# Sliding-window attention and a feed-forward layer on one core: PSUM banks by row tile, one phase of sums, output banks by row of tokens

## The chip, the cores and the metric

The kernel runs on one core of one Trainium2 chip. The metric is the device time of one execution in microseconds (us). Three executions of the kernel before took 361.39 to 361.45 us, the median is 361.41 us. Instructions are queued in order on five engines: TensorE (PE, with its weight loads listed apart as PEld), VectorE (DVE), ScalarE (ACT), GpSimd (POOL) and SyncE (SP). PE writes to PSUM, which has eight banks of 512 float32 columns on 128 partitions; DVE and ACT read it.

## The reference, cut to what matters

Eight batches of eight heads, 576 positions, head dimension 64; each position sees the positions up to 32 away. The result, as 4608 tokens of 512 values, goes through two matrices with a piecewise function between.

```python
scores = np.matmul(q, k.transpose(0, 1, 3, 2)) / np.sqrt(D)
mask = np.abs(pos[:, None] - pos[None, :]) <= 32
attn = softmax(np.where(mask, scores, -1e9))
x = np.matmul(attn, v)                 # -> tokens (4608, 512)
h = x @ w_in                           # (512, 2048)
g = np.where(h >= 1, h, np.where(h <= -1, 0.0, (h + 1) ** 2 / 4))
out = g @ w_out                        # (2048, 512)
```

## The kernel before

**Attention.** Heads come in pairs `h` (0 and 1), four pairs `y` per batch. Keys go in chunks `c` of 64, nine per head. For each chunk, `scores` multiplies 64 keys by the 128 queries around them (L194); ACT takes the exponent (L201), DVE or POOL multiplies with a band mask (L202), and the masked weights stay in `pt`. The last chunk has 96 queries and its own function `scores8` (L210, L213, L214). Every one of these matmuls uses a quarter of the PE array: 64 rows by 64 columns. The row half holds the head in `scores`; in the sums it holds the parity of the chunk.

**Sums.** `Sums` takes a range of queries (256, 224 or 96 wide) of two pairs of heads, or of four for the last 96, and forms for each head the sum of weights times `vn` and the sum of weights times `ones`, with 64 by 64 matmuls (L217) into a tile `bb` of two PSUM banks: bank 0 for the weighted sums, bank 1 for the row sums. Both row halves of the array add into each bank. So the work is in two phases: in phase 0 the low row half adds to bank 0 and the high half to bank 1, in phase 1 the other way round. Between the two stands a DVE copy of one number out of the bank, `scr` (L273), and phase 1 begins behind it. `end` takes the logarithm of the row sums (L280), the exponent of its negative (L281) and queues a DVE product (L283) that writes `xT`; `flush` issues it at the beginning of the next slot.

**Main loop.** 144 slots (`a`), eight for each tile of 256 tokens, and then slots that finish the output. A slot has eight matmuls of 256 columns (L392) into a bank `hp`, out of two banks in turn; ACT makes `rr` (L400), and DVE makes `gT` out of both (L401, L402). The second matrix follows `LAG` = 8 slots behind: four matmuls of 512 columns (L416) into `op`, one tile of two banks, one bank for each 128 tokens. Each slot gives two matmuls to either bank. In the eighth slot of a tile the first bank gets its last two matmuls, ACT copies it to `osb` (L420), then the second bank gets its two, and ACT copies that one; SP sends both out. The next tile needs `op` in the slot after.

**What sets the order.** `ev` holds for a slot which sums and which scores run there; the list `sl` gives 35 slots three or four apart, each with one `Sums` and, but for two of them, the `scores` of a later step. I call such a slot an event. In an event slot the program order is: the eight L392, phase 0, `scores`, phase 1, `end`, the four L416; an event with no scores puts phase 0 ahead of the L392. Slots 8 to 11 and 19 to 21 also transpose q and k of batches 1 and 2 on PE (L171): q, its copy by ACT, then k into the same PSUM tile, and its copy by DVE (L172). Batches 0 and 1 are loaded in long rows, two pairs of heads at a time (`load_long`), and put in order by a copy (`relay`, L145; batch 1 on POOL, queued behind the loads that POOL issues). All loads are issued from POOL and share a ring of semaphores.

**Before the first slot**, all scores of batch 0 and the sums of its first 256 queries run, in two `Sums`.

Of the kernel before, what the change touches and what calls it, by code (L numbers as in the profile page):

```python
# [15 lines left out]
def kernel(  # L16
# [19 lines left out]

# [34 lines left out]
    scr = const.tile([128, 8], FP, name="scr")  # L71
# [11 lines left out]
    def load_long(b, qd, t):  # L83

        src, dst, nm = ((q, qn, "qn"), (k, kn, "kn"))[t]
        if qd == 0:
            dst[b] = nat.tile([128, 2, 2, S], BF, name=nm, tag=nm)
        rows = src[b].rearrange("(h y) s d -> h (y s) d", h=2)[:, 2 * qd * S:2 * qd * S + 2 * S]
        nc.gpsimd.dma_start(out=dst[b][:, qd], in_=rows.rearrange("h (x j) d -> x h (j d)", j=NC))

    def load_nat(b, t):
        src, dst, nm = ((q, qn, "qn"), (k, kn, "kn"), (v, vn, "vn"))[t]
        x = dst[b] = nat.tile([128, NU, 2, D], BF, name=nm, tag=nm, bufs=3 if t == 2 else 2)
        for h in range(2):
            nc.gpsimd.dma_start(out=x[:, :, h], in_=src[b, NY * h:NY * h + NY].rearrange("y s d -> (y s) d")  # L95
                                .rearrange("(u p) d -> p u d", p=128))

# [27 lines left out]
    load_nat(0, 2)  # L125
# [9 lines left out]
    load_nat(1, 2)  # L135
# [19 lines left out]
    def tpose(b, n, t, copy, ps):  # L155
# [3 lines left out]
        if b < LONG:  # L159
            qd, part = divmod(n, 2)  # L160
            j0, j1 = ((0, 5), (5, 9))[part]
            src = (qj, kj)[t][b, qd]
            dst = o.rearrange("d (y p j) -> d y p j", p=64, j=NC)[:, 2 * qd:2 * qd + 2, :, j0:j1]
            i = ps[:, :j1 - j0].rearrange("d j (g p) -> d g p j", g=2)
# [7 lines left out]
        copy(dst, i)  # L172
# [9 lines left out]
    def half(n):  # L182
        return HD[n % 2]

    def scores(b, ys, cs, eng, pool=ps_s):

        if b not in pt:
            pt[b] = ptp.tile([128, 2, NY, 512], BF, name="pt")
        ps = two_banks(pool)
        n = 0  # L190
        for y in range(*ys):
            for c in range(2 * cs[0], 2 * cs[1]):
                for h in range(2):
                    nc.tensor.matmul(ps[half(NC * y + c), h, 128 * (n // 2):128 * (n // 2) + 128],  # L194
                                     kT[b][HD[h], S * y + 64 * c:S * y + 64 * c + 64],
                                     qTs[b % 3][HD[h], PAD + S * y + 64 * c - 32:PAD + S * y + 64 * c + 96],
                                     start=True, stop=True)
                n += 1
        p = pt[b][:, :, ys[0]:ys[1], 128 * cs[0]:128 * cs[1]]
        like = "p h (y j) -> p h y j"  # L200
        A.activation(p, ps[:, :, :64 * n].rearrange(like, y=ys[1] - ys[0]), AF.Exp, scale=D ** -0.5)  # L201
        eng.tensor_mul(p, p, mask4[:, :128 * n].rearrange("p (h j) -> p h j", h=2).rearrange(like, y=ys[1] - ys[0]))  # L202

    def scores8(b, eng):

        p = pt8[b] = ptp.tile([128, 2, 2 * TAIL], BF, name="pt8")
        ps = two_banks(ps_s)
        for y in range(NY):
            for h in range(2):
                nc.tensor.matmul(ps[half(y), h, TAIL * (y // 2):TAIL * (y // 2) + TAIL],  # L210
                                 kT[b][HD[h], S * y + 512:S * y + 576],
                                 qTs[b % 3][HD[h], PAD + S * y + MAIN:PAD + S * y + S], start=True, stop=True)
# [3 lines left out]
    def mm(o, w, x, first):  # L216
        nc.tensor.matmul(o, w, x, skip_group_check=True, start=first[0], stop=True)  # L217
        first[0] = False

    muls = []  # L220

    class Sums:


        def __init__(self, b, ys, lo, hi, pool=ps_n):
            self.b, self.ys, self.lo, self.hi = b, ys, lo, hi
            self.bb = two_banks(pool)
            self.firsts = [[[True], [True]], [[True], [True]]]

        def parts(self, y, par):  # L230

            b, lo, hi = self.b, self.lo, self.hi
            R = half(NC * y + par)
            if lo == MAIN:
                c = 7 if par else 8
                yield c, lo, lo + (64 if par else TAIL), lambda h: (
                    pt[b][R, h, y, 448:512] if par else pt8[b][R, h, TAIL * (y // 2):TAIL * (y // 2) + TAIL])
                return
            for c2 in range(4):
                a0, a1 = max(0, 128 * c2 - 32 + 64 * par, lo), min(128 * c2 + 96 + 64 * par, hi)  # L240
                if a0 < a1:
                    yield 2 * c2 + par, a0, a1, lambda h, a0=a0, a1=a1: (
                        pt[b][R, h, y, a0 + 32 - 64 * par:a1 + 32 - 64 * par])

        def phase(self, n):

            b, lo, hi = self.b, self.lo, self.hi
            todo = []
            for y in range(*self.ys):
                off = (y - self.ys[0]) * (hi - lo) - lo  # L250
                for lowhigh in range(2):
                    R = HD[lowhigh]
                    par = (NC * y + lowhigh) % 2
                    got = list(self.parts(y, par))
                    bank = n ^ lowhigh
                    if bank == 1 and len(got) > 1:
                        a0, a1 = got[0][1], got[-1][2]
                        got = [(None, a0, a1, lambda h, a0=a0, a1=a1, par=par, R=R, y=y: (
                            pt[b][R, h, y, a0 + 32 - 64 * par:a1 + 32 - 64 * par]))]
                    for m, (c, a0, a1, p) in enumerate(got):  # L260
                        for h in range(2):
                            w = ones[R] if bank else vn[b][R, (NC * y + c) // 2, h]
                            todo.append(((y, bank == 0 and m + 1 == len(got), m), bank, lambda bank=bank, h=h, w=w, p=p, a0=a0, a1=a1, off=off: mm(
                                self.bb[HD[h], bank, off + a0:off + a1], w, p(h), self.firsts[bank][h])))
            todo.sort(key=lambda x: x[0])
            if n:
                todo.reverse()
            for _, _, f in todo:
                f()
            if n == 0:  # L270

# [47 lines left out]
    x.phase(1)  # L319
    x.end()  # L320
    flush()
    x = Sums(0, (2, 4), 0, TB, ps_o)
    x.phase(0)
    scores8(0, V)
    x.phase(1)
# [134 lines left out]
```

## Time and profile before

| | |
|---|---|
| median of three runs | 361.41 us |
| the profiled execution, its own time | 363.6 us |
| its span, first to last instruction | 361.9 us |
| PE busy | 308.1 us, 85% |
| DVE busy | 246.7 us, 68% |
| ACT busy | 192.0 us, 53% |
| POOL busy | 126.4 us, 35% |

Times within the trace count from the start of the span. A row of the list of instructions in order of time begins with start and length in us, then engine, line, operation, output and inputs and a count; brackets behind it give the idle time of the engine before it and what ended that. The lengths of matmuls include a modelled end, so how fast a row of them goes is read from the starts of two rows that follow each other.

### The profile page before, as it was taken

What the parts mean: (1) busy time and instruction counts of PE and PEld (TensorE: products, weight loads), DVE (VectorE), ACT (ScalarE), POOL (GpSimd) and SP (SyncE); (2) the same over time, 40 slices, a digit from 0 to 9 for tenths busy, and PEclk for the clock granted to TensorE, in tenths of its full rate; (3) what the DMA queues carried; (4) which work ended last, traced back from release to release, by engine and by line L of the source; (5) the groups of instructions that cost most, each with busy time, mean ns of one, the idle gap of its engine ahead of it and who ended that gap; (6) DMA issues with size and microseconds to landing.
All of it is one profiled execution on the core that took longest, in us unless ns stands there. A gap on an engine that the chain in (4) does not pass through costs nothing.

```text
span 361.9 us, 8161 instructions
## 1 busy us (share of the span) xinstructions
PE 308.1 (85%) x3465; PEld 206.6 (57%) x3508; DVE 246.7 (68%) x398; ACT 192.0 (53%) x314; POOL 126.4 (35%) x106
## 2 busy tenths in 40 slices
PE   2667778777989898989898989899979899999985
PEld 1445555455666566656565656565646565655642
DVE  2648778566687768777687777786748777778750
ACT  2645437554556555557655566556454756543331
POOL 8655900141623482238321844139221242100000
PEclk9999999899999999999999999999989999999999
DMA  7999997192909999899981699109950101010111
GB/s 103 179 205 207 178 152 35 60 115 17 126 0 189 68 144 55 184 95 85 110 159 58 45 157 187 60 1 146 172 124 7 60 2 61 0 60 1 61 58 58
DMA packets 127845, 34.22 MB, mean 95 GB/s; under 512 B 117056, under 2 KB 123200, under 8 KB 127808
## 3 DMA queue, kind: packets, MB, share of 16 engines
q0 software_dynamic: 99264, 18.35, 67.7%
q1 hardware_dynamic: 28544, 15.34, 17.5%
q8 instruction: 27, 0.44, 0.5%
q14 instruction: 10, 0.08, 0.1%
HBM read 36.70 MB, written 9.44 MB: 127 GB/s over the span
## 4 chain that ended last, share of the span: by engine, by line
PE 70%; ACT 12%; DVE 10%; issue 6%; DMA 1%; POOL 0%; ACTq 0%; POOLq 0%
PE hp L392 32%; PE bb L416 30%; PE bb L217 6%; DVE hp L401 3%; ACT rr L400 3%; DVE gT L402 3%; ACT osb L420 3%; PE tp L171 2%; ACT qT L172 2%; ACT lr L280 1%; DVE scr L273 1%; DMA kn<-in_k_dram 1%; ACT rc L281 1%; ACT pt L201 1%; DVE xT L283 1%
## 5 line engine op out<-in xcount | busy, mean ns | idle before, releaser
L416 PE MATMUL bb<-w_out,gT 128*128 128x512 bf16 x533 | 143.9, 383 | 22.8 <-ACT osb L420 17.5
L392 PE MATMUL hp<-xT,w_in 128*128 128x256 bf16 x1152 | 154.2, 278 | 4.9 <-DVE gT L402 3.3
L400 ACT ACTIVATE rr<-hp 128x512 f32<-128x512 f32 x144 | 85.9, 597 | 130.6 <-PE hp L392 125.7
L392 PEld LDWEIGHTS <-w_in 128*128 128x128 bf16 x1152 | 113.7, 100 | 48.9 <-issue 4.6
L401 DVE TENSOR_TENSOR hp<-hp,rr 128x512 f32<-128x512 f32 x144 | 100.8, 700 | 57.6 <-ACT rr L400 54.8
L402 DVE SCALAR_TENSOR_TENSOR gT<-rr,hp 128x512 bf16<-128x512 f32 x144 | 99.0, 687 | 4.9
L202 POOL TENSOR_TENSOR pt<-pt,mask 128x1024 bf16<-128x1024 bf16 x24 | 51.2, 2133 | 116.6 <-ACT pt L201 110.3
L416 PEld LDWEIGHTS <-gT 128*128 128x128 bf16 x576 | 53.6, 98 | 62.1 <-issue 24.0
L283 DVE TENSOR_TENSOR xT<-bb,rc 128x512 bf16<-128x512 f32 (+2 forms) x40 | 25.5, 637 | 19.4 <-ACT rc L281 19.3
L217 PE MATMUL bb<-pt,vn 64*64 64x64 bf16 (+3 forms) x712 | 31.4, 213 | 6.7 <-DVE scr L273 4.6
L217 PEld LDWEIGHTS <-vn 64*64 64x64 bf16 x712 | 25.0, 111 | 18.0 <-issue 17.9
L201 ACT ACTIVATE pt<-bb 128x1024 bf16<-128x1024 f32 (+1 forms) x33 | 32.8, 997 | 1.7 <-PE bb L194 1.7
L420 ACT COPY osb<-bb 128x512 f32<-128x512 f32 x36 | 20.9, 582 | 19.4 <-PE bb L416 19.4
L217 PE MATMUL bb<-pt,ones 64*64 64x256 bf16 (+4 forms) x384 | 30.8, 257 | 0.0
L214 POOL TENSOR_TENSOR pt<-pt,mask 128x384 bf16<-128x384 bf16 x7 | 6.4, 915 | 56.6 <-ACT pt L213 56.6
L281 ACT ACTIVATE rc<-lr 128x512 f32<-128x512 f32 (+2 forms) x40 | 23.5, 587 | 1.3
L280 ACT ACTIVATE lr<-bb 128x512 f32<-128x512 f32 (+2 forms) x40 | 22.0, 551 | 2.6 <-PE bb L217 2.0
L95 POOL DMA_DIRECT2D vn<-in_v_dram x16 | 19.6, 1238 | 1.9 <-DMA w_out<-in_moe_w_out_dram 1.3
L194 PE MATMUL bb<-qT,kT 64*64 64x128 bf16 x512 | 13.6, 228 | 1.8 <-DVE qj L145 0.8
L95 POOL DMA_DIRECT2D qn<-in_q_dram x12 | 14.9, 1244 | 0.0
L95 POOL DMA_DIRECT2D kn<-in_k_dram x12 | 14.7, 1238 | 0.0
L217 PEld LDWEIGHTS <-ones 64*64 64x64 bf16 x384 | 13.6, 108 | 1.9 <-issue 1.9
(40 smaller groups left out, 92.2 us busy)
## 6 DMA issues: line engine op xcount, KB each, us to landing
out_dram<-osb SPq DMA_DIRECT2D x36, 256.0 KB, 2.0
qn<-in_q_dram POOLq DMA_DIRECT2D x16, 288.0 KB, 6.0
kn<-in_k_dram POOLq DMA_DIRECT2D x16, 288.0 KB, 8.0
vn<-in_v_dram POOLq DMA_DIRECT2D x16, 288.0 KB, 9.6
w_in<-in_moe_w_in_dram POOLq DMA_DIRECT2D x8, 256.0 KB, 10.8
w_out<-in_moe_w_out_dram POOLq DMA_DIRECT2D x4, 512.0 KB, 13.5
qT<-qn SPq DMA_TRANSPOSE x5, 5.9
kT<-kn SPq DMA_TRANSPOSE x5, 4.7
```

The lines of the kernel that those rows point to most:

```text
L95: nc.gpsimd.dma_start(out=x[:, :, h], in_=src[b, NY * h:NY * h + NY].rearrange("y s d -> (y s) d") .rearrange("(u p) d -> p u d", p=128))
L201: A.activation(p, ps[:, :, :64 * n].rearrange(like, y=ys[1] - ys[0]), AF.Exp, scale=D ** -0.5)
L202: eng.tensor_mul(p, p, mask4[:, :128 * n].rearrange("p (h j) -> p h j", h=2).rearrange(like, y=ys[1] - ys[0]))
L217: nc.tensor.matmul(o, w, x, skip_group_check=True, start=first[0], stop=True)
L281: A.activation(rc[:, :n], lr[:, :n], AF.Exp, scale=-1.0)
L283: muls.append(lambda: V.tensor_mul(xT[:, self.ys[0]:self.ys[1], r0:r0 + w], self.bb[:, 0, :n].rearrange("p (y j) -> p y j", y=ny), rc[:, : ...
L392: nc.tensor.matmul(hp[:, j], w_in[:, kk, 256 * f + 128 * j:256 * f + 128 * j + 128], xT[:, kk, r0:r0 + TB], start=kk == 0, stop=kk == 3)
L400: A.activation(rr, hp, AF.Relu, scale=0.5, bias=0.5)
L401: V.tensor_max(hp, hp, rr)
L402: V.scalar_tensor_tensor(gT[t][:, 2 * f:2 * f + 2], rr, 1.0, hp, op0=ALU.min, op1=ALU.mult)
L416: nc.tensor.matmul(op[:, tt], gT[t][:, ff, 128 * tt:128 * tt + 128], w_out[:, ff], start=ff == 0, stop=ff == 2 * NF - 1)
L420: A.copy(osb, op[:, tt])
```

## The change

In `sums`, which takes the place of the class, a row half of the array stands for one of two pairs of heads (`y1` and `y1 + 2`) in place of the parity of the chunk. Each row half has a bank of its own, with the weighted sums in the first columns and the row sums behind them. So there is one phase, no `scr` copy, and one stretch of matmuls in front of the scores. `scores`, `scores8`, the loads of q, k (batches 0 and 1) and v are re-laid to suit: those DMAs are split by halves of the partitions, two for each that was there.

`op` becomes a tile of one bank for 128 tokens, filled by sixteen matmuls in four slots in a row, out of two banks in turn; the copy to `osb` comes once in four slots. `LAG` goes from 8 to 12, `gT` has three buffers. In the slots before the twelfth, the two banks of `op` serve as third and fourth bank for `hp`. Before the first slot only those scores of batch 0 run that its first 256 queries need; the others go to slots 0 to 2, and the remaining sums to slots 3, 4 and 6 (before: 1, 1 and 4). The transposes of q and k in a slot are issued together, ahead of both copies.

```diff
-    def __init__(self, b, ys, lo, hi, pool=ps_n):
-            ...
-            if n == 0:
-                col = (self.ys[1] - self.ys[0]) * (hi - lo) - (1 if lo < MAIN else TAIL)
-                V.tensor_copy(scr[64:65, 0:1], self.bb[64:65, 0, col:col + 1])
+    def sums(b, y1, lo, hi, pool=ps_n):
+        bb = two_banks(pool)
+        ...
+        for n, (c, c0, c1, p) in enumerate(todo):
+            o = D0 if c is None else 0
+            for a in range(2):
+                for h in range(2):
+                    nc.tensor.matmul(bb[HD[h], a, o + c0:o + c1], ones[HD[a]] if c is None else vn[b][HD[a], c, h],
+                                     p(a, h), start=n == 0, stop=True, skip_group_check=True)
+        def end():
+            ...
+            A.activation(lr[:, :, :D0], bb[:, :, D0:2 * D0], AF.Ln)
+            A.activation(rc[:, :, :D0], lr[:, :, :D0], AF.Exp, scale=-1.0)
 ...
-    LAG = 8
+    LAG = 12
 ...
-    at(1, (0, (0, 2), TB, MAIN), None)
-    at(1, (0, (2, 4), TB, MAIN), None, ps_o)
-    at(4, (0, (0, NY), MAIN, S), None)
+    at(0, None, (0, (0, 2), (1, 2), (2, 4)))
+    at(1, None, (0, (0, 2), (0, 1), (3, 4)))
+    at(2, None, (0,))
+    at(3, (0, 0, TB, MAIN), None)
+    at(4, (0, 1, TB, MAIN), None)
+    at(6, (0, 0, MAIN, S), None)
 ...
-            hp = ps_h.tile([128, 2, TB], FP, name="hp", tag="hp")
+            if a < LAG and a % 4 > 1:
+                hp = ps_o.tile([128, 2, TB], FP, name="hp", tag="op")
+            else:
+                hp = ps_h.tile([128, 2, TB], FP, name="hp", tag="hp")
 ...
-            t, f = divmod(a - LAG, NF)
-            if f == 0:
-                op = two_banks(ps_o)
-            for tt in range(2):
-                for ff in (2 * f, 2 * f + 1):
-                    nc.tensor.matmul(op[:, tt], gT[t][:, ff, 128 * tt:128 * tt + 128], w_out[:, ff],
-                                     start=ff == 0, stop=ff == 2 * NF - 1)
-                if f == NF - 1:
+            for x in range(4 * (a - LAG), 4 * (a - LAG) + 4):
+                tt, ff = divmod(x, 2 * NF)
+                if ff == 0:
+                    op = ps_o.tile([128, DM], FP, name="op", tag="op")
+                nc.tensor.matmul(op, gT[tt // 2][:, ff, 128 * (tt % 2):128 * (tt % 2) + 128], w_out[:, ff],
+                                 start=ff == 0, stop=ff == 2 * NF - 1)
+                if ff == 2 * NF - 1:
                     osb = osp.tile([128, DM], FP, name="osb")
-                    A.copy(osb, op[:, tt])
+                    A.copy(osb, op)
 ...
-            for x in range(2):
-                tpose(b, n, x, (A.copy, V.tensor_copy)[x], tp[:, x])
+            copies = [tpose(b, n, x, (A.copy, V.tensor_copy)[x], tp[:, x]) for x in range(2)]
+            for x in copies:
+                x()
```

Two places show how the queues of ACT and DVE move. The first is ACT at slot 103, an event in which a tile of the output also ends (`pt` is the exponent of scores, `lr` and `rc` belong to the sums, `osb` to the output, `rr` to the slots). Before:

```order
L400 ACTIVATE rr<-hp 128x512 x4
L201 ACTIVATE pt<-bb 128x2x2x256
L280 ACTIVATE lr<-bb 128x512
L281 ACTIVATE rc<-lr 128x512
L420 COPY osb<-bb 128x512 x2
L400 ACTIVATE rr<-hp 128x512 x3
```

After, from the event of slot 99 to the one of slot 103:

```order
L210 ACTIVATE pt<-bb 128x2x2x256
L263 ACTIVATE lr<-bb 128x2x224
L264 ACTIVATE rc<-lr 128x2x224
L406 COPY osb<-op 128x512
L388 ACTIVATE rr<-hp 128x512 x4
L210 ACTIVATE pt<-bb 128x2x2x256
L263 ACTIVATE lr<-bb 128x512
L264 ACTIVATE rc<-lr 128x512
L406 COPY osb<-op 128x512
L388 ACTIVATE rr<-hp 128x512 x3
```

Two copies behind one event have become one copy every four slots; at this place it still stands behind the three of the event and ahead of the next `rr`.

The second is DVE in the slots 0 to 3, from the last product for `xT` before slot 0 on. Before:

```order
L283 TENSOR_TENSOR xT<-bb,rc 128x2x256
L401 TENSOR_TENSOR hp<-hp,rr 128x512
L402 SCALAR_TENSOR_TENSOR gT<-rr,hp 128x512
L273 COPY scr<-bb 1x1 x2
L401 TENSOR_TENSOR hp<-hp,rr 128x512
L402 SCALAR_TENSOR_TENSOR gT<-rr,hp 128x512
L283 TENSOR_TENSOR xT<-bb,rc 128x2x224 x2
L401 TENSOR_TENSOR hp<-hp,rr 128x512
L402 SCALAR_TENSOR_TENSOR gT<-rr,hp 128x512
```

After:

```order
L269 TENSOR_TENSOR xT<-bb,rc 128x2x256 x2
L389 TENSOR_TENSOR hp<-hp,rr 128x512
L390 SCALAR_TENSOR_TENSOR gT<-rr,hp 128x512
L211 TENSOR_TENSOR pt<-pt,mask_94 128x4x256
L389 TENSOR_TENSOR hp<-hp,rr 128x512
L390 SCALAR_TENSOR_TENSOR gT<-rr,hp 128x512
L211 TENSOR_TENSOR pt<-pt,mask_94 128x4x128
L389 TENSOR_TENSOR hp<-hp,rr 128x512
L390 SCALAR_TENSOR_TENSOR gT<-rr,hp 128x512
L225 TENSOR_TENSOR pt_417<-pt_417,mask_95 128x384
```

The `scr` copies are gone, the mask products of batch 0 have moved from ahead of slot 0 into the first slots, and the products for the later `xT` stand three slots further on.

## Rows read from the trace of the kernel before

**Rows 1.** The page's first part: busy us, share of the span, instructions.

```profile
PE 308.1 (85%) x3465; PEld 206.6 (57%) x3508; DVE 246.7 (68%) x398; ACT 192.0 (53%) x314; POOL 126.4 (35%) x106
```

**Rows 2.** Waits of PE: engine line waited for, total us, times, longest us.

```profile
PE bb L416 <- ACT osb L420: 17.5, 19, 1.7
PE tp L171 <- ACT qT L172: 6.0, 7, 0.9
PE bb L217 <- DVE scr L273: 4.6, 11, 1.7
PE hp L392 <- DVE gT L402: 3.3, 4, 1.5
```

**Rows 3.** PE in order of time, where an output tile ends without an event.

```profile
104.80 1.03 PE L416 MATMUL bb<-w_out,gT 128*128 128x512 bf16 x4
105.66 1.04 PE L392 MATMUL hp<-xT,w_in 128*128 128x256 bf16 x8
106.53 0.59 PE L416 MATMUL bb<-w_out,gT 128*128 128x512 bf16 x2
107.86 0.59 PE L416 MATMUL bb<-w_out,gT 128*128 128x512 bf16 x2 [0.73 <-ACT osb L420]
```

**Rows 4.** All engines in order of time: slot 103, event and end of tile.

```profile
262.46 0.24 PE L217 MATMUL bb<-pt,vn 64*64 64x128 bf16 x2
...
262.71 0.39 PE L194 MATMUL bb<-qT,kT 64*64 64x128 bf16 x16
...
262.95 0.16 DVE L273 COPY scr<-bb 1x1 f32<-1x1 f32 x1
263.16 0.24 PE L217 MATMUL bb<-pt,vn 64*64 64x128 bf16 x2
...
263.17 1.02 ACT L201 ACTIVATE pt<-bb 128x1024 bf16<-128x1024 f32 x1
...
263.74 0.38 PE L416 MATMUL bb<-w_out,gT 128*128 128x512 bf16 x1 [0.16 <-issue]
...
265.25 0.57 ACT L420 COPY osb<-bb 128x512 f32<-128x512 f32 x1
...
265.86 0.59 PE L416 MATMUL bb<-w_out,gT 128*128 128x512 bf16 x2 [1.75 <-ACT osb L420]
...
266.29 1.71 PE L392 MATMUL hp<-xT,w_in 128*128 128x256 bf16 x8
```

**Rows 5.** Busy us by stretch (counts), then granted clock, DMA share, GB/s.

```profile
260.00:270.00 10.00, 8.04 (x82) 4.89 (x81) 6.02 (x10) 4.94 (x8) 2.12 (x1) 0.83 0.72 120
```

**Rows 6.** PE in order of time at the end.

```profile
348.97 0.59 PE L416 MATMUL bb<-w_out,gT 128*128 128x512 bf16 x2 [0.78 <-ACT osb L420]
...
357.54 0.59 PE L416 MATMUL bb<-w_out,gT 128*128 128x512 bf16 x2 [0.67 <-ACT osb L420]
```

**Rows 7.** PE in order of time: slot 0 (its last six) and slot 23.

```profile
23.73 1.44 PE L392 MATMUL hp<-xT,w_in 128*128 128x256 bf16 x6 [1.60 <-DVE xT L283]
...
86.83 1.04 PE L392 MATMUL hp<-xT,w_in 128*128 128x256 bf16 x8
```

**Rows 8.** Groups by line and shape: count, busy us, mean ns, idle before.

```profile
L401 DVE TENSOR_TENSOR hp<-hp,rr 128x512 f32<-128x512 f32 x144 | 100.8, 700 | 57.6 <-ACT rr L400 54.8
L402 DVE SCALAR_TENSOR_TENSOR gT<-rr,hp 128x512 bf16<-128x512 f32 x144 | 99.0, 687 | 4.9
...
L217 PEld LDWEIGHTS <-vn 64*64 64x64 bf16 x712 | 25.0, 111 | 18.0 <-issue 17.9
...
L283 DVE TENSOR_TENSOR xT<-bb,rc 128x448 bf16<-128x448 f32 x16 | 10.0, 624 | 7.4 <-ACT rc L281 7.3
...
L101 POOL DMA_DIRECT2D w_in<-in_moe_w_in_dram x8 | 5.0, 641 | 2.6 <-DMA vn<-in_v_dram 2.6
...
L202 DVE TENSOR_TENSOR pt<-pt,mask 128x1024 bf16<-128x1024 bf16 x5 | 3.4, 686 | 0.3 <-ACT pt L201 0.3
...
L172 DVE COPY kT<-tp 128x640 bf16<-128x640 bf16 x4 | 3.3, 824 | 1.6 <-PE tp L171 1.6
```

More of the change, by code (lines that the diff above doesn't have):

```diff
@@ L96, in load_nat, with load_v @@
                                 .rearrange("(u p) d -> p u d", p=128))
+    def load_v(b):
+        x = vn[b] = nat.tile([128, 2 * NC, 2, D], BF, name="vn", tag="vn", bufs=3)
+        for h in range(2):
+            for a in range(2):
+                y = NY * h + 2 * a
+                nc.gpsimd.dma_start(out=x[64 * a:64 * a + 64, :, h], in_=v[b, y:y + 2].rearrange("y s d -> (y s) d")
+                                    .rearrange("(c r) d -> r c d", r=64))
     def load_w_in(n):
@@ L180, with scores @@
     HD = (slice(0, 64), slice(64, 128))
-    def half(n):
-        return HD[n % 2]
-    def scores(b, ys, cs, eng, pool=ps_s):
+    def scores(b, ys, pars, cs, eng, pool=ps_s):
         if b not in pt:
-            pt[b] = ptp.tile([128, 2, NY, 512], BF, name="pt")
+            pt[b] = ptp.tile([128, 2, 2, 2, 512], BF, name="pt")
         ps = two_banks(pool)
         n = 0
-        for y in range(*ys):
-            for c in range(2 * cs[0], 2 * cs[1]):
-                for h in range(2):
[L194 to L212, printed above, removed]
+        for y1 in range(*ys):
+            for par in range(*pars):
+                for c2 in range(*cs):
+                    c = 2 * c2 + par
+                    for a in range(2):
+                        for h in range(2):
+                            s0 = S * (y1 + 2 * a) + 64 * c
+                            nc.tensor.matmul(ps[HD[a], h, 128 * n:128 * n + 128], kT[b][HD[h], s0:s0 + 64],
+                                             qTs[b % 3][HD[h], PAD + s0 - 32:PAD + s0 + 96], start=True, stop=True)
+                    n += 1
@@ L213, in scores8 @@
         A.activation(p, ps[:, :, :2 * TAIL], AF.Exp, scale=D ** -0.5)
         eng.tensor_mul(p, p, mask8.rearrange("p (h j) -> p h j", h=2))
-    def mm(o, w, x, first):
-        nc.tensor.matmul(o, w, x, skip_group_check=True, start=first[0], stop=True)
-        first[0] = False
     muls = []
-    class Sums:
-        def __init__(self, b, ys, lo, hi, pool=ps_n):
[L226 to L269, printed above, removed]
-            if n == 0:
-                col = (self.ys[1] - self.ys[0]) * (hi - lo) - (1 if lo < MAIN else TAIL)
-                V.tensor_copy(scr[64:65, 0:1], self.bb[64:65, 0, col:col + 1])
-        def end(self):
-            ny, w = self.ys[1] - self.ys[0], self.hi - self.lo
-            n = ny * w
-            lr = smp.tile([128, 512], FP, name="lr", bufs=1)
-            rc = smp.tile([128, 512], FP, name="rc")
-            A.activation(lr[:, :n], self.bb[:, 1, :n], AF.Ln)
-            A.activation(rc[:, :n], lr[:, :n], AF.Exp, scale=-1.0)
-            r0 = (self.b * S + self.lo) % RING
-            muls.append(lambda: V.tensor_mul(xT[:, self.ys[0]:self.ys[1], r0:r0 + w],
-                                             self.bb[:, 0, :n].rearrange("p (y j) -> p y j", y=ny),
-                                             rc[:, :n].rearrange("p (y j) -> p y j", y=ny)))
@@ L376 @@
             relay(*x, P)
-        for x in loads.get(a, []):
-            load_nat(*x)
+        for b, x in loads.get(a, []):
+            load_nat(b, x) if x < 2 else load_v(b)
         flush()
-        todo = [(Sums(*sums, pool) if sums else None, sc) for sums, sc, pool in ev.get(a, [])]
-        for x, sc in todo:
-            if x and not sc:
-                x.phase(0)
         if t < NB:
```

183 lines of the change are left out of this document (114 added, 69 removed).

## The prediction

> **What bounds the kernel now.** I first read the busy shares [rows 1]: PE is busy 308.1 of 361.9 us, no other engine reaches 250. The time is PE's, so I looked next at what PE waits for [rows 2]: 17.5 us for the copies of finished output tiles, 6.0 for the copy between the transposes of q and k, 4.6 for `scr`, 3.3 for `gT`. Then I read stretches in order of time, to see what a wait costs by the starts of the rows.
>
> A plain slot is 0.86 us of L392-to-L416 either way: 104.80 to 105.66 for four L416, 105.66 to 106.53 for eight L392 [rows 3]. So 256 columns take 0.109 us, 2.35 columns per ns, and a slot is 1.73 us. No engine but PE needs that long: DVE's two instructions take 0.70 and 0.69 us [rows 8].
>
> Where an output tile ends, two L416 stand at 106.53 and the next two at 107.86 [rows 3]; without the wait they would follow after 0.43. The stop costs 0.90 us, more than the 0.73 named as idle, which counts from a modelled end. Where an event falls into the same slot, ACT reaches the copy only behind the exponent and both instructions of the sums, at 265.25, though PE could go on at 263.96; PE goes on at 265.86 [rows 4], a loss of 1.90. There the matmuls behind it are slow too: the eight L392 at 266.29 take 1.71 instead of 1.04, and the granted clock of the ten us is 0.83 [rows 5], so PE fell from 2.4 to 1.2 GHz for about a third of them. That costs 10 x (1 - 0.83) = 1.7 us.
>
> In an event, phase 0 starts at 262.46, the scores at 262.71, phase 1 at 263.16 [rows 4]. Sixteen scores of 128 columns, four side by side, are 512 columns, 0.22 us; they have 0.45. The `scr` copy ends at 263.11 and phase 1 follows it: 0.23 us are lost to that copy, although the list of waits names only a part.
>
> **The change part by part.** I count from slot 23 at 86.83 [rows 7], where the steady part begins, and take the beginning apart.
>
> *Output banks.* The first matmul on a bank now comes four slots, 6.9 us, after the bank was finished; ACT's longest queue, an event and a copy, is under 3.5 us [rows 4]. So none of these waits should be left. Of the 19 [rows 2], 18 lie behind slot 23: twelve ordinary ones of 0.90, three late ones (slots 23, 39, 103) of 1.75 to 1.90, and three at the end, where the tail has only L416 left, the first and last of them in [rows 6], 0.87 each. That is 10.8 + 5.4 + 2.6 = **18.8 us**. The slow clock behind the one at slot 103, **1.7 us**, should go with it. One copy is left behind the last matmul as before.
>
> *One phase.* 31 events lie behind slot 23, in groups of five. Three of five have sixteen scores, 0.23 each. One has eight of 96 columns, which hide 0.09 of the same 0.45: 0.36. One is the last 96 queries, with 28 matmuls instead of 32: 0.3. Six groups of 1.35, and one event more: **8.3 us**. Lengths and columns of the other sums stay the same, as do the changes between quarter and whole-array matmuls. DVE loses the 0.16 us of `scr`, which nobody else waited for.
>
> What could spoil this is the order. Now four matmuls of one shape follow each other, two on the low row half, two on the high, and then the next four. [Rows 4] show phase 0 with 14 matmuls, 512 columns for a row half, in 0.25 us; at 2.35 columns per ns the columns alone are 0.22. So the weight loads are hidden there, though several pairs on the same row half follow each other. The Trainium skill says otherwise ("TensorE: Matmul & The Clock Gate", Part 3, The mechanism): a weight load overlaps running matmuls only where the row group differs. By that rule, the loads of the new order would stand open; the trace speaks against it, and the price is a rival below.
>
> *LAG.* The first 12 slots have no L416, where before it was 8, and four groups more stand in the tail, where nothing hides them: 4 x 0.86 = **+3.45 us**. What the shorter slots 8 to 11 give back is in the beginning.
>
> *A wait that may come up.* With the waits gone, events follow faster, and `hp` has two banks: the L392 of a slot wait for the `gT` of two slots before. After an event ACT does exponent, logarithm, exponent, 0.9 + 0.6 + 0.5 from 263.17 to 265.25 [rows 4], then `rr` of the next slot, 0.6; DVE does `xT`, 0.62, then 1.39 [rows 8]. Counted from the event slot's first L392, now 2.6 us long, `gT` of the next slot is ready at about 6.0 us; the L392 that wait for it would start at 6.06. It just fits. Where an output copy stands in the same slot, 0.57 [rows 4] come in between: 0.45 late. This is so in six events behind slot 23 (23, 35, 39, 59, 99, 103): **+2.7 us**, bounds 0 and 14 (all 31). The mask product on POOL, needed three slots later, has two us to spare.
>
> *The beginning.* Before, slot 0 runs from 23.73 and slot 23 from 86.83 [rows 7]. Ahead of slot 0 there are now 40 scores instead of 72, but both copies of a `kT` half have come to share one tile and wait for each other, and each load is two DMAs; a DMA for 64 partitions still costs POOL 0.64 us [rows 8] where one for 128 would do. I take 0.6 us off slot 0, bounds +1 and -2. From there DVE sets the pace, since PE may run up to four banks ahead. From the first L401, near 25.4, to the last `kT` copy of slot 11 DVE has 12 x 1.42 for the slots (with 0.03 between), 1.4 for mask products, 1.8 for three `xT`, 3.1 for four `kT` copies [rows 8]: 23.3; 1.2 more for waits in the first slots and between the copies, which go ACT, then DVE, then the next transposes. That is 50. Slots 12 to 15 have mask products on DVE: 4 x (1.42 + 0.69) and an `xT`, 9.1; slot 16 needs the `xT` of the sums of slot 15, through ACT and DVE, 2.8 more: 61.9. From slot 16 PE leads: 7 x 1.73, two events of 0.75, three slots with transposes. These lose 0.86 of waiting each, 6.0 over 7 [rows 2], and cost 0.75: 15.9 in all, slot 23 at 77.8. As PE will have stood for some 2 us before slot 16, I add one fall of the clock of the size of [rows 5], 1.7: 79.5. **7.3 us** are gained, bounds 0 and 11. The upper bound on time is POOL: the copies of batch 1 stand behind all loads, at most eight of which are in flight, and these are half as large now; I expect these copies some 6 us later, just in time.
>
> The sum against the span: 361.9 - 18.8 - 1.7 - 8.3 + 3.45 + 2.7 - 7.3 = 332.0. The profiled execution took 363.6, 1.7 more than its span; the median of the runs, 361.4, is 0.5 less than it. I predict the median: **331.5 us**.
>
> **The rivals.**
> - *ACT and DVE become the bound at every event.* For: the margin above is 0.06 us. Against: [rows 2] show PE waiting for `gT` four times, though slots without an event give the margin back. Every event at 0.45: 14 instead of 2.7, 343.
> - *The beginning gives nothing*, because DVE is late, POOL's copies later than thought, or the clock low for long: PE is given less work in these slots. 331.5 + 7.3 = 339.
> - *Weight loads stand open in the new order.* Six or seven rounds of 0.11 us [rows 8] in each of 31 events, 0.7 each, 22 us: 353. Against it stands phase 0 in [rows 4]. This is the Trainium skill's rule named above.
> - *The output banks don't free PE*: the copy comes so late that four slots don't cover it. Only with ACT 7 us behind; 350.
> - *The four quarters don't run side by side* and the time ends above 361. All four now add up in two banks at once. In turn, the 3300 to 4100 columns of an event take 1.4 to 1.75 us instead of 0.35 to 0.44, 1.2 more; over 35 events 42 us: 373. It decides from 30/35 = 0.85 us per event on. Against: the scores have a bank per row half already, and 16 of them pass in under 0.4 us [rows 4].
> - *Better than thought*: no fall of the clock, no new waits, slot 0 earlier: 326.
>
> **How the numbers follow.** Forecast 0.58 (326.5 to 337), bound by ACT and DVE 0.15, no gain at the beginning 0.10, better 0.08, open weight loads 0.04, banks don't help 0.03, slower 0.02. The range from 325 to 343 takes in the first four and leaves out 0.09 and some tails. Faster by over 0.2% (about what a measurement can tell from none) 0.97, within 0.2% 0.01, slower 0.02.
>
> **What would show it.** PE should have no wait for `osb` except near the end, none for `scr`; an event should take 0.85 us from the end of its L392 to the first L416 instead of 1.07 to 1.15; slot 23 should start near 79.5; PE should be over 90% busy from there. Waits of L384 (the new L392) for `gT` should sum to about 3 us behind slot 23. If PE's busy time per event grows, the order of loads was wrong; if slot 23 comes after 85, the beginning was; if the waits for `gT` pass 10, ACT and DVE are the bound.

## The result and the profile after

| | before | after | predicted |
|---|---|---|---|
| median, lowest and highest of the runs | 361.43 (361.39 to 363.35) us | 331.10 (330.98 to 331.37) us | 331.5 us |
| the profiled execution | 363.6 us | 331.08 us | |
| its span | 361.9 us | 329.4 us | 332.0 us |

The changed kernel takes 0.915 of the time before (95% interval 0.912 to 0.918). The forecast is 0.4 us off, but its span is 2.6 off: two errors cancel, so that it came this close is luck. The section on the terms finds them.

The page's first part, as [rows 1]:

```profile
PE 294.4 (89%) x3435; PEld 200.5 (61%) x3476; DVE 237.0 (72%) x359; ACT 191.5 (58%) x314; POOL 138.4 (42%) x130
```

Waits of PE, as [rows 2] (what waits, for what; us in total, times, longest):

```profile
PE tp L179 <- DVE qj L153: 5.9, 1, 5.9
...
PE hp L384 <- DVE xT L269: 3.9, 3, 1.7
...
PE tp L179 <- DVE kT L180: 2.4, 3, 0.8
...
PE bb L257 <- POOL pt L211: 0.7, 1, 0.7
...
PE hp L384 <- DVE gT L390: 0.6, 3, 0.3
```

The 17.5 us for `osb` and the 4.6 for `scr` have no row any more. Of the waits for other engines, all that is left stands in the first 63 us, but for the last two rows: a wait for POOL's mask product, which is new, and three short ones for `gT`, at 155.80, 235.44 and 243.72 (before, the four of [rows 2] all stood in the first 41 us).

A tile of the output ends in slot 31, PE in order of time, as [rows 3]:

```profile
94.00 1.04 PE L384 MATMUL hp<-xT,w_in 128*128 128x256 bf16 x8
94.88 1.03 PE L402 MATMUL op<-w_out,gT 128*128 128x512 bf16 x4
95.74 1.04 PE L384 MATMUL hp<-xT,w_in 128*128 128x256 bf16 x8
```

The slot is 1.74 us long, as one in which no tile ends. Slot 103 is an event with an output copy, as in [rows 4]; this is what follows its scores, on PE, ACT and DVE:

```profile
239.07 1.02 ACT L210 ACTIVATE pt<-bb 128x1024 bf16<-128x1024 f32 x1 [0.17 <-PE bb L203]
...
239.99 0.59 ACT L263 ACTIVATE lr<-bb 128x512 f32<-128x512 f32 x1
...
240.61 0.63 ACT L264 ACTIVATE rc<-lr 128x512 f32<-128x512 f32 x1
...
241.15 0.57 ACT L406 COPY osb<-op 128x512 f32<-128x512 f32 x1
...
241.56 1.04 PE L384 MATMUL hp<-xT,w_in 128*128 128x256 bf16 x8
241.61 0.60 ACT L388 ACTIVATE rr<-hp 128x512 f32<-128x512 f32 x1
...
242.25 0.70 DVE L389 TENSOR_TENSOR hp<-hp,rr 128x512 f32<-128x512 f32 x1 [0.28 <-ACT rr L388]
...
242.98 0.69 DVE L390 SCALAR_TENSOR_TENSOR gT<-rr,hp 128x512 bf16<-128x512 f32 x1
...
243.72 1.05 PE L384 MATMUL hp<-xT,w_in 128*128 128x256 bf16 x8 [0.27 <-DVE gT L390]
```

PE goes past the copy without a stop, but ACT does four instructions before the `rr` of slot 104. Its `gT` ends at 243.67, and the L384 of slot 106 start behind it, at 243.72, 0.43 late.

Granted clock (the number behind POOL's share), where it was 0.83 in [rows 5], and around slot 16, where the prediction added a fall:

```profile
50.00:60.00 10.00, 8.45 (x150) 5.54 (x153) 8.34 (x13) 6.82 (x10) 1.80 (x3) 1.00 2.56 129
60.00:70.00 10.00, 7.94 (x110) 5.52 (x111) 6.59 (x10) 6.14 (x12) 4.04 (x4) 1.00 0.25 39
...
240.00:250.00 10.00, 9.58 (x98) 6.39 (x98) 7.52 (x12) 6.76 (x13) 3.05 (x2) 1.00 0.45 102
```

It stayed at 2.4 GHz in all three. PE does stop in slot 16, as the prediction had it, in the changed kernel

```profile
62.01 0.92 PE L384 MATMUL hp<-xT,w_in 128*128 128x256 bf16 x7 [1.75 <-DVE xT L269]
```

and, nearly as long, in the kernel before at the end of slot 15, where the clock did fall:

```profile
65.21 1.01 PE L416 MATMUL bb<-w_out,gT 128*128 128x512 bf16 x2 [1.69 <-ACT osb L420]
```

```profile
65.00:70.00 5.00, 4.79 (x26) 2.70 (x29) 1.71 (x3) 1.34 (x3) 0.00 (x0) 0.66 0.28 105
```

The profiled execution of the kernel before has three falls to 1.2 GHz, at 34, 65 and 267 us, the changed one has only the first (at 35), apart from the last microseconds of each. The end, as [rows 6], has a row of matmuls without a stop:

```profile
319.66 5.99 PE L402 MATMUL op<-w_out,gT 128*128 128x512 bf16 x26
```

The bulk of slot 0 and slot 23, as [rows 7]:

```profile
23.41 1.65 PE L384 MATMUL hp<-xT,w_in 128*128 128x256 bf16 x7 [0.92 <-DVE xT L269]
...
77.50 1.04 PE L384 MATMUL hp<-xT,w_in 128*128 128x256 bf16 x8
```

So slot 23 comes 9.3 us earlier than before, and from there to the end of the span it takes 251.9 us instead of 275.1.

### The profile page after: what moved, and what is told of

Same layout as the page of the kernel before. It is cut to its first block, busy times and chain, and to the rows that moved or that the text cites. A ratio compares the mean times of both kernels' runs of the same rounds, so it can differ in the third digit from the quotient of the medians.

```text
span 329.4 us, 8115 instructions
## 1 busy us (share of the span) xinstructions
PE 294.4 (89%) x3435; PEld 200.5 (61%) x3476; DVE 237.0 (72%) x359; ACT 191.5 (58%) x314; POOL 138.4 (42%) x130
## 4 chain that ended last, share of the span: by engine, by line
PE 67%; POOL 8%; DMA 8%; ACT 7%; issue 5%; DVE 3%; ACTq 0%; POOLq 0%
PE op L402 30%; PE hp L384 29%; PE bb L257 5%; DMA w_out<-in_moe_w_out_dram 4%; ACT pt L210 2%; DMA kn<-in_k_dram 2%; DMA w_in<-in_moe_w_in_dram 2%; POOL vn L102 2%; PE bb L203 2%; PE tp L179 1%; ACT rr L388 1%; DVE hp L389 1%; DVE gT L390 1%; ACT osb L406 1%; POOL pt L211 1%
## 5 line engine op out<-in xcount | busy, mean ns | idle before, releaser
L384 PE MATMUL hp<-xT,w_in 128*128 128x256 bf16 x1152 | 152.6, 276 | 5.3 <-DVE xT L269 3.9
L402 PE MATMUL op<-w_out,gT 128*128 128x512 bf16 x535 | 138.2, 379 | 5.7 <-issue 5.2
L384 PEld LDWEIGHTS <-w_in 128*128 128x128 bf16 x1152 | 112.3, 99 | 49.7 <-DVE gT L390 7.4
L402 PEld LDWEIGHTS <-gT 128*128 128x128 bf16 x576 | 53.3, 98 | 42.1
L269 DVE TENSOR_TENSOR xT<-bb,rc 128x512 bf16<-128x512 f32 (+1 forms) x32 | 21.0, 658 | 22.0 <-ACT rc L264 21.9
L406 ACT COPY osb<-op 128x512 f32<-128x512 f32 x36 | 20.9, 581 | 14.7 <-PE op L402 14.3
L102 POOL DMA_DIRECT2D vn<-in_v_dram x32 | 27.5, 894 | 1.8 <-DMA w_out<-in_moe_w_out_dram 1.8
L257 PE MATMUL bb<-pt,ones 64*64 64x256 bf16 (+3 forms) x352 | 20.5, 263 | 5.6 <-DVE xT L269 2.9
L257 PEld LDWEIGHTS <-ones 64*64 64x64 bf16 x352 | 11.1, 110 | 13.8 <-issue 11.5
L257 PE MATMUL bb<-pt,vn 64*64 64x128 bf16 (+3 forms) x712 | 19.2, 210 | 0.0
L257 PEld LDWEIGHTS <-vn 64*64 64x64 bf16 x712 | 17.6, 112 | 0.0
```

Of the source, the lines that this page charges most:

```text
L102: nc.gpsimd.dma_start(out=x[64 * a:64 * a + 64, :, h], in_=v[b, y:y + 2].rearrange("y s d -> (y s) d") .rearrange("(c r) d -> r c d", r=64))
L257: nc.tensor.matmul(bb[HD[h], a, o + c0:o + c1], ones[HD[a]] if c is None else vn[b][HD[a], c, h], p(a, h), start=n == 0, stop=True, skip_g ...
L384: nc.tensor.matmul(hp[:, j], w_in[:, kk, 256 * f + 128 * j:256 * f + 128 * j + 128], xT[:, kk, r0:r0 + TB], start=kk == 0, stop=kk == 3)
L402: nc.tensor.matmul(op, gT[tt // 2][:, ff, 128 * (tt % 2):128 * (tt % 2) + 128], w_out[:, ff], start=ff == 0, stop=ff == 2 * NF - 1)
L406: A.copy(osb, op)
```

## The experiments

All are the changed kernel with the edit shown. The slots are starts of their first matmul in the trace, so that a part of the kernel can be read as a difference. Slots and span are those of one profiled execution, which took 363.6 us for before, 355.89 for op_pair and 337.02 for tpose_old.

| kernel | median us (lowest to highest) | slot 0 | slot 23 | slot 143 | span |
|---|---|---|---|---|---|
| before | 361.43 | 21.52 | 86.83 | 346.72 | 361.9 |
| after | 331.10 | 22.12 | 77.50 | 313.39 | 329.4 |
| op_pair | 354.32 (351.53 to 355.89) | 22.45 | 79.56 | 335.68 | 354.2 |
| two_phases | 339.42 (339.01 to 339.71) | 23.02 | 79.77 | 321.59 | 337.6 |
| lag8 | 329.35 (329.16 to 329.47) | 23.14 | 79.39 | 315.28 | 327.8 |
| rows_apart | 338.49 (338.38 to 338.57) | 22.32 | 78.77 | 320.68 | 336.7 |
| two_hp | 330.82 (330.67 to 331.01) | 22.09 | 77.05 | 312.95 | 329.0 |
| tpose_old | 335.67 (335.36 to 337.02) | 23.07 | 83.42 | 319.32 | 335.3 |
| no_ln | 328.68 (328.47 to 328.92) | 21.23 | 76.52 | 310.78 | 326.8 |
| lag6w | 329.03 (328.85 to 331.08) | 22.91 | 79.12 | 316.38 | 327.3 |
| lag7w | 327.22 (326.75 to 327.84) | 22.29 | 77.83 | 313.66 | 325.3 |
| lag7_mix | 325.81 (325.55 to 326.01) | 22.26 | 77.79 | 312.69 | 324.3 |

After, op_pair, two_hp, lag8 and tpose_old issue the same work ahead of slot 0; still it starts between 22.09 and 23.14. It follows the last load of `kn` of batch 0: the `relay` copy (`kj`, DVE) behind that load starts at 12.84 in the changed kernel, 12.81 in two_hp, 13.01 in op_pair, 13.76 in lag8 and 13.79 in tpose_old, and slot 0 comes 9.3 to 9.4 later in each. Why the load lands up to 1 us later is open, so I compare from slot 0 on.

**op_pair**: the output tile as before.

```diff
-            for x in range(4 * (a - LAG), 4 * (a - LAG) + 4):
-                ...
+            t, f = divmod(a - LAG, NF)
+            if f == 0:
+                op = two_banks(ps_o)
+            for tt in range(2):
+                for ff in (2 * f, 2 * f + 1):
+                    nc.tensor.matmul(op[:, tt], ...)
+                if f == NF - 1:
+                    ...
+                    A.copy(osb, op[:, tt])
```

> The changed kernel with its output tile as in the kernel before: one tile of two banks, two matmuls to either bank in a slot, both copies in the eighth slot; LAG stays 12. Theory (the output-bank term of the prediction): with LAG 12 the tiles end in slots 19, 27, 35 and so on. Twelve ordinary waits at 0.90, three behind an event (35, 59, 99) at 1.9, two in the tail at 0.87, and slot 19: 10.8 + 5.7 + 1.7 + 1.0 to 1.9, so +19 to +20, up to 1.7 more where the clock falls, and up to 1.7 less where the small waits for gT go: 348 to 352 us. Rival 1 (in the faster kernel other waits end later, and hide these copies): under 340. Rival 2 (the copies cost more, because the engines are busier now): over 354.

The wait is back, and the clock falls behind the events 59 and 99 (waits of PE; then stretches, with the granted clock behind POOL's share):

```profile
PE bb L407 <- ACT osb L411: 18.3, 19, 2.1
```

```profile
160.00:170.00 10.00, 9.68 (x89) 6.07 (x90) 4.81 (x8) 4.91 (x9) 4.19 (x3) 0.83 1.91 188
...
240.00:250.00 10.00, 7.01 (x74) 4.55 (x74) 4.90 (x8) 4.67 (x9) 5.55 (x4) 0.79 2.20 157
250.00:260.00 10.00, 9.84 (x98) 6.28 (x97) 6.11 (x9) 4.68 (x8) 1.67 (x1) 0.87 0.66 124
```

By starts, ten of the twelve ordinary ends cost 0.89 to 0.94 and two 1.0; the three behind an event cost 1.85, 2.35 and 2.65; the tail is 2.5 longer. That is 20.3 us. The slots 60, 100 and 101 lose 4.0 more at the low clock (in all the three stretches lose 1.7 + 2.1 + 1.3 = 5.1 to it, the rest in the events' own slots), and 1.8 of small waits for `gT` are gone: 22.5 of the 22.7 that this kernel takes longer from slot 23 to the end. The theory is right in the places of the waits and in the ordinary ones. The three behind an event cost 6.85 where it had 5.7, and the tail 2.5 where it had 1.7. The median lies over the top of its range, by these and by the clock, for which I had allowed 1.7: of the four runs the two at a mean clock of 0.995 took 351.5 and 353.1, the two at 0.977, one of which is the trace read here, 355.6 and 355.9. Rival 1 is out. The median lies in the range of rival 2 (over 354), whose dearer copies are there only behind the events, 1.15 in all.

**two_phases**: the sums in two halves around the scores, with the `scr` copy between.

```diff
-        for n, (c, c0, c1, p) in enumerate(todo):
-            ...
+        part(0, cut)
+        x = D0 + todo[cut][1]
+        V.tensor_copy(scr[64:65, 0:1], bb[64:65, 0, x:x + 1])
         ...
         def end():
+            part(cut, len(todo))
```

> The changed kernel with two phases put back: half of the matmuls of the sums, a copy of one number out of the bank by DVE (ahead of the slot's other DVE work), the scores, then the other half. Columns, banks and loads stay. Theory (the one-phase term): 0.23 for an event with 16 scores, 0.36 with eight, 0.3 for the last 96 queries, so +8.3 over 31 events, 0.8 more in slots 14 to 19, and up to 1.7 less because the small waits for gT fade: 338 to 340 us. Rival 1 (the gain came from the new layout, not from the stop between): under 333. Rival 2 (DVE reaches the copy late, since PE now runs closer behind DVE): over 343.

An event, PE and DVE in order of time:

```profile
93.20 0.29 PE L262 MATMUL bb<-pt,ones 64*64 64x224 bf16 x4
...
93.42 0.39 PE L204 MATMUL bb<-qT,kT 64*64 64x128 bf16 x16
...
93.65 0.16 DVE L267 COPY scr<-bb 1x1 f32<-1x1 f32 x1
93.86 0.28 PE L262 MATMUL bb<-pt,ones 64*64 64x192 bf16 x4
```

The scores take 0.44 from start to start again, though their columns need 0.22. The 31 event slots from slot 23 on sum to 87.26 us instead of 79.52: 7.74, or 0.25 each. From slot 23 to slot 143 only 5.9 of it show, because none of the small waits for `gT` is left. The theory holds, both in size and in that exchange.

**lag8**: `LAG = 8`.

> The changed kernel with LAG 8 in place of 12, nothing else changed (two of four slots take a bank of the output for hp up to slot 7). Theory (the LAG term): the tail loses four groups of 0.86, 3.45; slots 8 to 11 get them, where PE waits 0.6 to 0.8 us in each for the kT copies, so all but about 0.5 is hidden there; the output needs the last quarter of w_out in slot 11, which lands near 49 us, 1 to 2 us late: 327.5 to 329.5 us. Rival (those slots are PE's, or the landing of w_out holds up everything behind it): 330.5 or more.

From slot 143 to the end it takes 12.5 us instead of 16.0, which is the 3.45 of the term. Slots 0 to 23 take 56.25 instead of 55.38; in part this is the row

```profile
PE op L402 <- DMA w_out<-in_moe_w_out_dram: 0.5, 1, 0.5
```

So LAG 12 costs 2.6 net by the trace. By the medians it is 1.75; slot 0 was 1.0 later here. The theory's place and size hold.

**rows_apart**: first the low row half of the array, then the high one.

```diff
-        for n, (c, c0, c1, p) in enumerate(todo):
-            o = D0 if c is None else 0
-            for a in range(2):
+        for a in range(2):
+            for n, (c, c0, c1, p) in enumerate(todo):
+                o = D0 if c is None else 0
                 for h in range(2):
```

> The changed kernel with the matmuls of the sums in another order: all of the low row half, then all of the high half, so that two quarters of the array run side by side in place of four. Same matmuls, loads, banks. Theory (in the changed kernel four quarters run side by side and the loads are hidden): the 0.32 to 0.47 us of the sums double, +0.3 to +0.45 in each of 35 events, less up to 1.7 of small waits that fade: 341 to 346 us. Rival 1 (the quarters don't run side by side, the row halves take turns in any order): 331 to 333. Rival 2 (a load is hidden only behind a matmul of the other row half): each of 12 to 14 pairs then shows about 0.11 more, 1.3 to 1.5 in an event, 45 us on top: over 375.

The event costs only 0.2 more (31 event slots: 85.56 us instead of 79.52), less than I expected. PE in order of time, from the sums to the first L402, here and then in the changed kernel at the same event (the traces lack the record of the first of the four L402 of an event, so the row shown is the second):

```profile
92.28 0.28 PE L257 MATMUL bb<-pt,ones 64*64 64x224 bf16 x2
92.41 0.26 PE L257 MATMUL bb<-pt,vn 64*64 64x96 bf16 x4
92.46 0.29 PE L257 MATMUL bb<-pt,ones 64*64 64x224 bf16 x4
92.58 0.26 PE L257 MATMUL bb<-pt,vn 64*64 64x96 bf16 x8
92.67 0.22 PE L203 MATMUL bb<-qT,kT 64*64 64x128 bf16 x1
92.67 0.25 PE L257 MATMUL bb<-pt,ones 64*64 64x192 bf16 x2
...
92.84 0.39 PE L203 MATMUL bb<-qT,kT 64*64 64x128 bf16 x11
93.39 0.38 PE L402 MATMUL op<-w_out,gT 128*128 128x512 bf16 x1 [0.16 <-issue]
```

```profile
90.68 0.29 PE L257 MATMUL bb<-pt,ones 64*64 64x224 bf16 x4
90.80 0.27 PE L257 MATMUL bb<-pt,vn 64*64 64x96 bf16 x8
90.90 0.25 PE L257 MATMUL bb<-pt,ones 64*64 64x192 bf16 x4
90.98 0.26 PE L257 MATMUL bb<-pt,vn 64*64 64x128 bf16 x8
91.06 0.40 PE L203 MATMUL bb<-qT,kT 64*64 64x128 bf16 x16
91.62 0.38 PE L402 MATMUL op<-w_out,gT 128*128 128x512 bf16 x1 [0.16 <-issue]
```

In the changed kernel the sums pass in 0.385 us, four at a time: each quarter of the array has 832 columns, 0.35 us at the rate of [rows 3], and the four in turn would take 1.4. In the other order the second 224-column pair, which is the first of the high half, starts at 92.46, with six matmuls of the low half still to start (two of 192 columns at 92.50 among them, in the same row). And a score starts at 92.67, ahead of sums that stand before it in the queue. So the two halves run side by side even when the queue holds them one after the other, and only part of the loss comes about. So the theory missed the size, and both rivals are out; for the changed kernel, four at a time is shown.

**two_hp**: `ps_h` for every `hp`, so no third and fourth bank in the first twelve slots.

> The changed kernel with two hp banks in all slots (the banks of the output tiles are not lent to the first twelve). Theory (the banks let PE run ahead, so that DVE is never without work in the first slots): with two banks the L384 of a slot wait for the gT of two slots before, then come 0.9 us of matmuls and 0.6 of rr, while DVE has 1.4 for the slot between; 0.2 to 0.4 in each of slots 2 to 11, more where sums or scores stand in it, and slot 23 falls 1 to 4 us later: 332 to 335 us. Rival (the pace of the first slots is DVE's either way, or that of the loads): 330.5 to 331.6.

A miss: the median is 0.3 us lower, and slots 0 to 23 take 54.96 instead of 55.38. The rival holds, though not which of its two reasons; the extra banks gain nothing.

**tpose_old**: the copy of q again between the transposes of q and k.

```diff
-            copies = [tpose(b, n, x, (A.copy, V.tensor_copy)[x], tp[:, x]) for x in range(2)]
-            for x in copies:
-                x()
+            for x in range(2):
+                tpose(b, n, x, (A.copy, V.tensor_copy)[x], tp[:, x])()
```

> The changed kernel with the old order of the transposes: q, its copy, k, its copy. Theory: in slots 19 to 21, where PE leads, 0.86 each as in the kernel before, 2.6 us; in slots 8 to 11, where a chain through the copies sets the pace, the transposes of k and two hops come into that chain, 0.3 to 0.4 each, 1.4 us: +4, 333.5 to 336.5 us. Rival 1 (slots 8 to 11 are held by the loads and by DVE, so nothing there): +2.6, 333.2 to 333.8. Rival 2 (all hidden in waits for other things): 331.

A row of the waits of PE, and PE in order of time from slot 20 to slot 21:

```profile
PE tp L179 <- ACT qT L180: 6.6, 7, 1.3
```

```profile
74.77 1.04 PE L384 MATMUL hp<-xT,w_in 128*128 128x256 bf16 x8
...
77.90 0.49 PE L179 MATMUL tp<-ident,kn 128*128 128x128 bf16 x6 [0.89 <-ACT qT L180]
...
78.23 1.04 PE L384 MATMUL hp<-xT,w_in 128*128 128x256 bf16 x8
```

From the start of slot 8 to that of slot 12 it takes 10.70 instead of 9.20, as the theory had it (1.4), but slot 12 gives 0.57 of that back. Slots 19 to 23 take 13.19 instead of 9.63: 3.56, not 2.6. From 74.77 to 78.23 it is 3.46 a slot instead of 2.41; the wait named is 0.89, the loss 1.05. In slot 19, where ACT comes late from an event, it is 1.46.

**no_ln**: the exponent takes the row sums.

> The changed kernel without the logarithm L263 (the exponent takes the row sums themselves; the output is then not the attention's). ACT has 0.6 us less in each event. Theory (the small waits for gT behind slot 23 come from ACT's queue of an event: exponent, logarithm, exponent, and a copy): about ten stretched groups, 1.7 us in all, go; ahead of slot 0 two logarithms stood in the chain to xT, up to 1.2 us: 328.0 to 329.5 us, and PE shows no wait of L384 for gT. Rival (those waits are DVE's, which has xT between its slots): the waits stay, and only the start moves: 329.8 to 330.5.

The waits for `gT` are gone: behind slot 23 no slot without an event is stretched by more than 0.05 us, and slots 23 to 143 take 1.63 less. The theory holds, the rival (DVE alone) doesn't.

**lag6w** and **lag7w**: `LAG = 6` and `LAG = 7`, and

```diff
-    load_v(1)
     load_w_out(3)
+    load_v(1)
```

> LAG 6 in place of 12, and the last quarter of w_out loaded ahead of the v of batch 1. Theory (from the run with LAG 8, 329.35: the tail gives 0.86 a slot, the first slots hide what they get, and there w_out was 0.7 late in slot 11): two tail slots less, 1.7, less 0.4 for the last gT, which the tail then needs two slots behind its matmuls, and 0.5 for w_out: 327 to 328.3 us. Rival (slots 6 to 9 are full, or the later v holds up the first sums of batch 1): 329.3 or more.

> LAG 7 in place of 12, the last quarter of w_out ahead of the v of batch 1 (as in the run with LAG 6). Theory (a wait for gT comes two slots behind each event whose slot also has an output copy, and nowhere else): LAG 12 and 8 have the copy in slots 3 mod 4, LAG 6 in 1 mod 4, LAG 7 in 2 mod 4, which meets the events 26, 42, 62, 106 and 110 only. So stretched slots at 28, 44, 64, 108 and 112 and at no other place, 0.2 to 0.45 each, 1.5 us in all as against 3.0 with LAG 6; the tail is one slot shorter than with LAG 8: 328.2 to 329.0 us. Rival (the stretched slots stand where they stood with LAG 6, or in slots of no such rule): 329 or more.

LAG 6 missed its range, and its time lies below that of the rival too: the tail got shorter as expected, but slots 23 to 143 took 1.4 more than with LAG 12. The slots without an event that are stretched (by more than 0.1 us over the 1.737 of a plain slot) say why:

| kernel | slots with output copies | events among them | stretched slots, us |
|---|---|---|---|
| after, LAG 12 | 3 mod 4 | 23, 35*, 39, 59, 99, 103 | 25 .21, 41 .22, 61 .32, 101 .32, 105 .43 |
| lag6w | 1 mod 4 | 29, 45, 49, 65, 69*, 73, 77, 81, 113 | 31 .32, 47 .32, 51 .43, 67 .43, 75 .28, 79 .32, 83 .32, 115 .32 |
| lag7w | 2 mod 4 | 26, 42, 62, 106*, 110 | 28 .32, 44 .33, 64 .32, 112 .27 |
| no_ln, LAG 12 | 3 mod 4 | as after | none |

Each stands two slots behind an event with an output copy, and moves with the copies. The exceptions, marked *, are events with the eight scores of 96 columns, whose exponent is 0.49 us instead of 1.02. So the rule of the run with LAG 7 holds but for its slot 108. Its time is under its range: slots 0 to 23 are as short as with LAG 12, 55.54, where I had taken the 56.2 of lag8 and lag6w, and slot 0 came 0.6 to 0.9 earlier than in those two.

**lag7_mix**: as lag7w, with two `hp` banks, and

```diff
-            loads.setdefault(a + t, []).append((b, t))
+            loads.setdefault(a + 3 * t, []).append((b, t))
```

> As the run with LAG 7, and also two hp banks in all slots, and the loads of q, k and v of a batch three slots apart in place of one, so that POOL has a mask product between two of them. Theory: the wait of the sums in slot 99 for POOL's mask product, 0.7 to 0.9, goes; two banks give 0.3 as they did alone: 1.0 to 1.3 less than with LAG 7 alone, 327.0 to 328.0 us. Rival (a later v or k holds up something else, or POOL's wait moves to another event): no better than LAG 7 alone.

In the changed kernel the only wait for POOL is in slot 99:

```profile
224.07 1.02 ACT L210 ACTIVATE pt<-bb 128x1024 bf16<-128x1024 f32 x1
...
224.41 3.44 POOL L102 DMA_DIRECT2D vn<-in_v_dram  x4
...
227.80 2.21 POOL L211 TENSOR_TENSOR pt<-pt,mask 128x1024 bf16<-128x1024 bf16 x1
...
230.06 0.29 PE L257 MATMUL bb<-pt,ones 64*64 64x224 bf16 x4 [0.72 <-POOL pt L211]
```

`pt` is there at 225.09, but POOL is busy with issuing the four DMAs of `vn` until 227.85. With the loads apart, slot 99 is 2.55 us long instead of 3.34 to 3.35. The median is 1.4 under that of LAG 7 alone, and under its range, as that was; of the 1.4, 0.8 is slot 99. The two banks show no gain here (slots 0 to 23 take 55.53 in both traces), and the rest was not separated. It is the fastest kernel here: 0.902 of the time before (0.896 to 0.908).

## Why the prediction was right, term by term

- **What bounds, and the output banks (18.8 us): right.** No wait for `osb` is left, and its undoing brings back 20.3 us of waits by starts, at 0.89 for an ordinary one where the sum had 0.90. The rival that the banks don't free PE is out.
- **One phase (8.3): right**, 7.7 when undone. With sixteen scores an event slot is 0.82 us (224 columns) to 0.90 (256) longer than a plain one, with the last 96 queries or the eight short scores 0.75 to 0.77, where the prediction had 0.85. It named that figure "from the end of its L392 to the first L416", but its 1.07 to 1.15 for the kernel before are this same difference of slot lengths. The Trainium skill's rule against it ("TensorE: Matmul & The Clock Gate", Part 3, The mechanism: a load overlaps matmuls only where the row group differs) did not come true: in the trace of rows_apart the low half alone goes from a pair of 96 columns at 92.405 to the next pair at 92.448, 43 ns, which is what the columns need.
- **LAG (3.45): right**, 3.5 in the tail of lag8.
- **The wait that may come up (2.7): right in mechanism and place, too large.** Five of the six named events make it, at 0.21 to 0.43 instead of 0.45; the sixth has the short exponent. All stretched slots sum to 1.8. What I had wrong was POOL: "two us to spare" left out the load of v, whose two DMAs have become four and hold POOL for 3.44 us, where the two of the kernel before held it for 2.46; the wait is 0.8 in slot 99. That POOL's issuing of the loads is the cause is shown by lag7_mix; that the split alone would do it is worked out from the 1 us between 3.44 and 2.46, and was not tried by itself.
- From slot 23 on these terms, with the 1.7 for the slow clock at slot 103, made 22.65; the traces give 275.1 - 251.9 = 23.2.
- **The beginning (7.3): right up to one term, the added fall of the clock; it was 9.3.** The prediction's way to slot 23 can be followed in the trace of the changed kernel: the last `kT` copy of slot 11 ends at 50.35 (predicted: 50), the L384 of slot 16 that wait for `xT` start at 62.01 (61.9), and slot 23 starts at 77.50 (77.8 without the fall). So 1.7 of the 2.0 us are the fall that was added because PE stands before slot 16, and 0.3 is the rest. PE does stand there, for 1.75 us, but the granted clock stayed at 1.00. One stop of that length doesn't say whether the clock falls: in the kernel before, stops of 1.69 and 1.75 (slots 15 and 103) were followed by a fall, and two of 1.59 (slots 23 and 39) were not. What decides it was not settled. The transposes that stay cost 0.67 in slots 20 and 21 (2.41 less 1.74), taken at 0.75.
- What the 9.3 consist of, as far as the runs say: undoing the transposes costs 4.97 from slot 0 to 23, the output banks 1.73, one phase 1.37, LAG 0.87, together 8.9; the rows of slot 0's bulk and slot 23 give 63.1 before and 54.1 after, 9.0. This is no proof that nothing else counts: two_hp gave 0.4 the other way, and the fall at 65 us of the kernel before, the split loads and the scores moved behind slot 0 were not undone. "PE may run up to four banks ahead" explained nothing: two banks do as well. The 0.86 for a transpose of the kernel before, from the list of waits, is too small (3.56 for three slots when undone, 0.89 named and 1.05 lost in slot 20), but the sum doesn't rest on it. Slot 0 itself came 0.3 earlier, not 0.6, a difference that is smaller than the 1 us by which slot 0 varies.
- **From span to median (-0.5): wrong.** The time is 1.7 us (1.65 to 1.77) more than the span in every execution seen, of all kernels. The profiled execution of the kernel before had a mean granted clock of 0.986; in the runs of that kernel beside these experiments, 0.999 went with 359.0 to 359.8 us, 0.995 with 360.6 to 361.2, 0.988 to 0.992 with 361.5 to 362.7, and 0.986 with 362.6 to 364.4. I took the slow clock at slot 103 off the sum, and then the 2.2 us by which the median lies under that execution. By these rows that counts much the same falls twice; the clocks of the three runs behind the median of 361.41 are not on record, so it isn't shown. The changed kernel took 331.1 both at 0.993 and at 1.000.

So the span was 2.6 too long, 1.7 by the fall that didn't come, 0.3 by the rest of the beginning and 0.6 from slot 23 on, and the step to the median 2.2 too short: 332.0 - 2.6 + 1.7 = 331.1.

## What to carry to other kernels

Cost a stop by the starts of the rows on both sides of it, in every term. Write down which falls of the clock the profiled execution has before its time is set beside a median, and give a fall that a stop might bring a chance and not a place in the sum. When a sum goes by points on the way (here the last copy of slot 11, slot 16, slot 23), look these up afterwards: they tell which term was off. Where a release of banks takes a stop away, look at once at the queue behind the same engine's long groups of instructions: here a copy of 0.57 us in the wrong slot decides whether the next but one slot is late, and the distance between two pipelines (`LAG`) moves it there or away. A DMA that is split in two costs its issuing engine more (for v, 3.44 us of POOL instead of 2.46), and whatever is queued behind it there waits for that.

## What the hardware showed that was not expected

The two row halves of the array work off their matmuls apart: a matmul of the high half started while six ahead of it in the queue, for the low half, had not (rows_apart, 92.46). The Trainium skill ("TensorE: Matmul & The Clock Gate", Part 3, The mechanism) says that matmuls start strictly in program order; here they don't. And the kernel before, with its stops of 1.6 to 1.8 us, took 359.0 to 364.4 us on one chip, longer the lower the mean granted clock (0.999 to 0.986), where the four runs of the changed one stay within 0.4. The clock is not all of it: lag7w took 326.8 to 327.8 with 1.000 in all four.
